# Attention and expert routing in one kernel: where the one-hot operands lie, when the last pair is routed, and how far the list products stand apart

## The chip, the cores and the metric

The kernel runs on one core of a Trainium2 chip. The metric is device time in microseconds (us) of one execution; the span in the profile runs from the first to the last instruction of that execution. The engines are named as in the profile: PE (TensorE), DVE (VectorE), ACT (ScalarE), POOL (GpSimd) and SP (SyncE, which here only issues transfers).

## The reference

Attention over 8 batches, 8 heads, 576 tokens and head size 64: heads 0 to 3 with a local window of 32, heads 4 to 7 with a stride of 32. Its 4608 token rows of 512 go through a mixture of 8 experts, of which each token takes one, and are scaled by its gate.

```python
mask_local = (rel >= 0) & (rel < stride)
mask_strided = (rel >= 0) & (pos[None, :] % stride == pos[:, None] % stride)
...
attn_out = np.matmul(attn, v)                       # softmax under the mask of the head
x = attn_out.transpose(0, 2, 1, 3).reshape(B * S, H * D)
logits = x @ w_gate + modality_bias[modality_id]
e_idx = np.argmax(logits, axis=1)
gate_w = probs[np.arange(N), e_idx]                 # probs: softmax of logits
for e in range(E):
    mask = e_idx == e
    h = np.maximum(x[mask] @ w1[e], 0.0)            # 512 -> 1024
    out[mask] = gate_w[mask, None] * (h @ w2[e])    # 1024 -> 512
```

## The kernel before

**Attention.** The batches are worked on in four pairs (1152 tokens each), each in eight units, local and strided heads in turn. The loop over n emits, for unit n, the scores, for n - 2 the transposes, for n - 3 the products with the values. A local unit writes its heads as columns of the pair's token rows `xt` (128 partitions x 9 x 528 floats, two buffers); a strided unit writes transposed rows `xc2`, `xc3` (two buffers each). `xc0` and `xc1` have one buffer each.

**Routing of a pair** (`after`, `finish_pair`, `route`). When a pair's last unit is done, its local columns are transposed into `xc0`, `xc1` (tiles `xl`, PE and ACT), the gate products run (`lg`), the strided rows are transposed back into `xt` (`xs`), the logits are turned (`lt`), and a chain of small DVE instructions finds expert, gate and rank of each token. Three transfers by SP write the rows with their token number and gate from `xt` to `xd` in memory (L543); the products `rk` give each token a block (`key`) and a place in it (`low`).

**Tables** (`slots`). The expert work is done in slots of 256 tokens of one expert. Phase 0 (2 slots) is built from the first two pairs, phase 1 (4 slots) from three, phase 2 (the other 12 of the 18 fixed slots, a half slot and slots run on demand) from all. For each pair q a `pick` makes one-hot operands: for each of nine token columns a 128 x 128 comparison of `low` with 0..127 (`place`, L702), and the hits of `key` on the slots' keys (`hit`, `tile_no`, L696 and L698, scaled by ACT in L700). Nine products (L718, tile `lists`) then give the token numbers of each slot; `lf` and `li` turn them into whole numbers. In phase 0 the operands lie in tiles of a pool that the expert stage uses later; in phases 1 and 2 in the tags `xc0` to `xc3`.

**Expert slots** (`ffn`). Each slot k has eight steps f of 12 + 6 products. ACT and DVE split the weights `raw` into `wh` and `wl`; the products `o` lag two steps. Before slot k + 1, its rows are gathered by POOL (`gather`, tile `fx`), copied by DVE at f = 1 (`rows`, L837), transposed by transfers on SP (`cols`, L840), copied again at f = 5 (`xs`, L849) and split into `xh`, `xl`. `rows` and `xs` are pinned to program order; so are a few other instructions.

**Order.** Routing and tables are generators in a list `extra`. `pop(k)` advances them by k steps, the oldest first; at `yield LATER` it goes on with the next generator, or ends if there is none. It is called with 5 in each attention step n and with 2 in each step f of a slot but f = 1 and f = 5. In the attention stage PE runs in the order of the program; all else is ordered by a planner, which lets an instruction run as soon as its own model of the times has it ready, the earlier in the program first. A tile with fewer buffers than uses waits until the earlier use is over. Each engine then works through its order without overtaking.

Of the kernel before, what the change touches and what calls it, by code (L numbers as in the profile page):

```python
# [11 lines left out]
F32 = mybir.dt.float32  # L12
F32R = mybir.dt.float32r
BF16 = mybir.dt.bfloat16
# [6 lines left out]
P = 128  # L21
B, H, S, D = 8, 8, 576, 64
STRIDE = 32
NBP = 4
T2 = 2 * S
# [4 lines left out]
SLOT = 256  # L30
# [4 lines left out]
ROW = DM + 16  # L35
WARM = 13
SETUP = 6
POPS, POPF = 5, 2
LT, PK, PL = 7, 2, 2
PT = (9, 9, 5)  # L40
LATER = 1
LAG = 2
SEND, SPLIT = 1, 5
# [131 lines left out]
def attention_moe(ctx: ExitStack, tc: tile.TileContext, a, out):  # L175
# [7 lines left out]
    def pa(name):  # L183
        return ps.tile([P, 512], F32, tag="a", name=name)
# [67 lines left out]
    ap = ap_cm.__enter__()  # L252
    pre_cm = tc.tile_pool(name="pre", bufs=2)
    pre = pre_cm.__enter__()
# [307 lines left out]
    def smalls(shape, dt, name):  # L562
        return cp.tile(shape, dt, name=name)
# [31 lines left out]
    def slots(ph):  # L595
# [4 lines left out]
        bp, n = PHASES[ph]  # L600
        last = ph == len(PHASES) - 1
        tiles = 9 * (bp + 1)
        nk = 2 * n + last
        ct = pa(f"ct{ph}")[:, 0:E]
        nc.tensor.matmul(ct, cb[:, M_ONE:M_ONE + P], cnt[:, bp + 1, :], start=True, stop=True)
        sh = [P, n, E]
# [11 lines left out]
        for sft in (1, 2, 4):  # L618
            t = smalls([P, E], F32, f"inc{ph}{sft}")
# [49 lines left out]
        if not last:  # L669

            t = smalls([P, E], F32, f"tk{ph}")
# [5 lines left out]
            for j in range(2):  # L677
                weights(wi, 0, j, True)

        picks = {}  # L680

        def pick(q, t0, tn):
            if t0 == 0:
                if ph == 0:
                    both = pre.tile([P, 4 * SLOT], F32R, tag=("xh", "xl")[q], name=f"pk{ph}{q}")
                else:
                    c = q if last else q % 2
                    both = ap.tile([P, T2], F32, tag=f"xc{c}", bufs=1 if c < 2 else 2, name=f"pk{ph}{q}")
                both = both.bitcast(BF16)
                picks[q] = (both[:, 0:9 * P].rearrange("p (t c) -> p t c", t=9),  # L690
                            both[:, 9 * P:9 * P + 18 * nk].rearrange("p (t v k) -> p t v k", t=9, v=2))
            place, eq = picks[q]
            ts = slice(9 * q + t0, 9 * q + t0 + tn)
            sh = [P, tn, nk]
            hit, tile_no = eq[:, t0:t0 + tn, 0, :], eq[:, t0:t0 + tn, 1, :]
            nc.vector.tensor_tensor(  # L696
                hit, key[:, ts].unsqueeze(2).to_broadcast(sh), ks.unsqueeze(1).to_broadcast(sh), ALU.is_equal)
            nc.vector.tensor_tensor(  # L698
                tile_no, hit, cf[:, C_V + ts.start:C_V + ts.stop].unsqueeze(2).to_broadcast(sh), ALU.mult)
            nc.scalar.activation(hit, hit, AF.Copy, scale=cf[:, C_P:C_P + 1])  # L700
            for i in range(t0, t0 + tn):
                nc.vector.tensor_scalar(  # L702
                    place[:, i, :], cb[:, M_IO:M_IO + P], low[:, 9 * q + i:9 * q + i + 1], None, ALU.is_equal)

        for _ in range(PK):
            yield LATER
        lists = pa(f"lists{ph}")[:, 0:2 * nk]
        steps = [(q, t0) for q in range(bp + 1) for t0 in range(0, 9, PT[ph])]
        done = 0
        for i in range(len(steps) + PL):  # L710
            if i < len(steps):
                q, t0 = steps[i]
                pick(q, t0, min(PT[ph], 9 - t0))
            yield LATER
            while done <= bp and i + 1 >= PL + sum(q <= done for q, _ in steps) - 1:
                place, eq = picks[done]
                for t in range(9):
                    nc.tensor.matmul(  # L718
                        lists, place[:, t, :], eq[:, t, :, :].rearrange("p v k -> p (v k)"),
                        start=(done == 0 and t == 0), stop=(done == bp and t == 8))  # L720
                done += 1
        lf = smalls([P, nk], F32, f"lf{ph}")
        nc.vector.tensor_scalar(lf[:], lists[:, nk:2 * nk], float(NT), None, ALU.add)
        li = smalls([P, nk], I32, f"li{ph}")
# [187 lines left out]
    for bp in range(NBP):  # L912
        xt = ap.tile([P, 9, ROW], F32, tag="xt", bufs=2, name=f"xt{bp}")
# [6 lines left out]
    tables = {}  # L920

    def after(bp, xt, xcs):
        while bp == NBP - 1 and 1 not in tables:
            yield LATER
        yield from finish_pair(bp, xt, xcs)
        yield
        for ph, (last_bp, _) in enumerate(PHASES):
            if bp == last_bp:
                tables[ph] = yield from slots(ph)
                if ph == 0:  # L930
                    gather(0)
                    yield LATER
                    gather(1)
# [14 lines left out]
    for ph, (bp, n) in enumerate(PHASES):  # L948
        last = ph == len(PHASES) - 1
# [59 lines left out]
    for k, (n, *_) in enumerate(plan):  # L1009
        def between(f):  # L1010
            if f not in (SEND, SPLIT):
                pop(POPF)
            if k + 1 < len(plan):
                if f == SEND:
                    sent[k + 1] = send_tokens(fp, plan[k + 1][0], gathered[k + 1])
                if f == SPLIT:
                    turned[k + 1] = split_tokens(fp, plan[k + 1][0], *sent[k + 1])
            elif f == 3:
                turn(k + 1)
            if f == 4:  # L1020
                gather(k + 2)

        ffn(fp, n, *turned[k], between, partial(load, k + 1))
# [4 lines left out]
    li, _, inc, wall = tables[len(PHASES) - 1]  # L1028
# [38 lines left out]
```

## Time and profile before

| | |
|---|---|
| time, median of 3 runs | 637.94 us (634.6 to 639.87) |
| the profiled execution | 637.19 us, of which span 635.4 us |
| instructions | 15373 |
| PE busy | 592.8 us, 93% |
| DVE busy | 453.0 us, 71% |
| ACT busy | 386.3 us, 61% |
| POOL busy | 191.7 us, 30% |
| mean granted clock of PE | 0.959 |
| moved by DMA | 102.55 MB |

A row of a time line gives start, length, engine, line, operation, output <- inputs, count, and in brackets the idle time before it with what ended it. A row of the waits gives total, number and longest. A row of stretches gives the stretch, its length, the busy time (and count) of PE, PEld, DVE, ACT and POOL, the clock granted to PE (1.00 is full), the share of the DMA engines that was busy, and GB/s. PE's products overlap, so their single lengths add up to more than the time that they take. The attention stage ends at about 171 us; then come 18 slots and the half slot.

### The profile page before, as it was taken

How to read it: one execution, taken by the hardware profiler on the slowest of the kernel's cores; microseconds unless marked ns; L12 is line 12 of the kernel's file. 1: busy time of each engine (PE TensorE's matmuls, PEld its weight loads, DVE VectorE, ACT ScalarE, POOL GpSimd, SP SyncE). 2: the span in 40 equal slices, each digit the busy share in tenths (PEclk: the TensorE clock that was granted, in tenths of full speed). 3: DMA queues.
4: the chain of work that ended last, by engine and by line, in shares of the span. 5: the costliest groups of instructions: out<-in, count | busy, mean ns of one | idle time of the engine just before them, and what ended most of it. 6: DMA issues, size and time to landing. Idle time of an engine off the chain costs nothing.

```text
span 635.4 us, 15373 instructions
## 1 busy us (share of the span) xinstructions
PE 592.8 (93%) x6057; PEld 516.9 (81%) x6057; DVE 453.0 (71%) x1185; ACT 386.3 (61%) x785; POOL 191.7 (30%) x169
## 2 busy tenths in 40 slices
PE   7989989879779978698999999999999999999995
PEld 4778868667668867597998999989999899998985
DVE  7765957847966659956868768777776876877642
ACT  5668677656736645545666666666666666666642
POOL 1010000012034404532553454354244245323311
PEclk9889979959969999889999999999999999999998
DMA  8986996996814487085585485243044148413531
GB/s 310 303 258 197 300 273 209 324 306 178 306 35 136 113 188 246 10 202 143 122 191 185 101 212 186 50 101 76 26 102 101 10 101 242 164 35 67 173 126 53
DMA packets 68079, 102.55 MB, mean 161 GB/s; under 512 B 46431, under 2 KB 47711, under 8 KB 64416
## 3 DMA queue, kind: packets, MB, share of 16 engines
q1 hardware_dynamic: 50848, 52.21, 31.8%
q0 software_dynamic: 16864, 48.83, 24.7%
q8 instruction: 49, 0.80, 0.5%
q10 hardware_dynamic: 288, 0.46, 0.3%
q14 instruction: 30, 0.25, 0.1%
HBM read 123.71 MB, written 19.43 MB: 225 GB/s over the span
## 4 chain that ended last, share of the span: by engine, by line
PE 75%; DVE 10%; DMA 6%; issue 4%; ACT 3%; SPq 0%; POOL 0%; POOLq 0%; DVEq 0%; ACTq 0%
PE h L867 29%; PE o L881 27%; DMA cols<-rows 5%; PE s L307 3%; PE o L339 3%; DVE wl L903 3%; PE ss L394 2%; PE xl L205 2%; PE ot L439 1%; PE t L205 1%; PE lg L485 1%; PE ts L205 1%; DMA qks<-in_qks 1%; PE s L303 1%; PE xs L205 1%
## 5 line engine op out<-in xcount | busy, mean ns | idle before, releaser
L903 DVE TENSOR_TENSOR wl<-raw,wh 128x512 fp32r<-128x512 f32 x288 | 186.9, 687 | 80.5 <-ACT wh L902 80.4
L902 ACT CAST wh<-raw 128x512 fp32r<-128x512 f32 x288 | 163.9, 619 | 94.2 <-PE o L881 94.2
L867 PE MATMUL h<-xh,wh 128*128 128x256 f32 x576 | 166.0, 288 | 5.2 <-ACT xh L854 4.0
L750 POOL DMA_INDIRECT raw<-in_w,wi x72 | 95.0, 1320 | 242.6 <-DVE wl L903 175.4
L867 PE MATMUL h<-xh,wl 128*128 128x256 f32 x576 | 165.2, 287 | 0.6 <-DVE wl L903 0.6
L867 PE MATMUL h<-xl,wh 128*128 128x256 f32 x576 | 164.5, 286 | 0.7 <-DVE xl L855 0.7
L867 PEld LDWEIGHTS h<-xh,wh 128*128 128x128 f32 x576 | 110.6, 192 | 12.6 <-ACT xh L854 4.9
L867 PEld LDWEIGHTS h<-xl,wh 128*128 128x128 f32 x576 | 111.0, 193 | 7.4 <-DVE xl L855 1.2
L881 PE MATMUL o<-wh,hh 128*128 128x512 f32 x288 | 115.6, 401 | 0.4 <-ACT hh L870 0.4
L881 PE MATMUL o<-wl,hh 128*128 128x512 f32 x288 | 113.8, 395 | 0.0
L881 PE MATMUL o<-wh,hl 128*128 128x512 f32 x288 | 113.6, 396 | 0.0
L867 PEld LDWEIGHTS h<-xh,wl 128*128 128x128 f32 x576 | 110.6, 192 | 1.4 <-DVE wl L903 0.8
L870 ACT ACTIVATE hh<-h 128x256 fp32r<-128x256 f32 x144 | 55.3, 384 | 51.2 <-PE h L867 51.2
L872 DVE SCALAR_TENSOR_TENSOR hl<-h,hh 128x256 fp32r<-128x256 f32 x144 | 60.5, 420 | 14.4 <-ACT hh L870 14.4
L881 PEld LDWEIGHTS o<-wh,hl 128*128 128x128 f32 x288 | 54.4, 189 | 12.4
L881 PEld LDWEIGHTS o<-wh,hh 128*128 128x128 f32 x288 | 54.5, 189 | 8.4 <-ACT hh L870 0.6
L881 PEld LDWEIGHTS o<-wl,hh 128*128 128x128 f32 x288 | 54.5, 189 | 5.9
L889 POOL DMA_INDIRECT out<-y,le x36 | 42.8, 1188 | 32.3 <-ACT y L888 25.9
L734 POOL DMA_INDIRECT fx<-xd,li x36 | 41.3, 1148 | 25.3 <-DVE li L725 13.5
L849 DVE COPY xs<-cols 128x1024 uint16<-128x1024 uint16 x34 | 24.4, 769 | 17.5 <-DMA cols<-rows 17.5
L307 PE MATMUL s<-qk,qd 128*64 128x64 f32 x576 | 25.7, 236 | 3.8 <-issue 3.1
L854 ACT CAST xh<-xs 128x512 fp32r<-128x512 f32 x34 | 19.3, 616 | 16.2 <-DVE xs L849 16.2
(182 smaller groups left out, 732.3 us busy)
## 6 DMA issues: line engine op xcount, KB each, us to landing
xd<-xt SPq DMA_DIRECT2D x12, 792.0 KB
qk<-in_qkl SPq DMA_DIRECT2D x16, 592.0 KB
qks<-in_qks SPq DMA_DIRECT2D x16, 576.0 KB
vv<-in_vl SPq DMA_DIRECT2D x16, 520.0 KB
vs<-in_vs SPq DMA_DIRECT2D x16, 288.0 KB
raw<-in_w,wi POOLq DMA_INDIRECT x72, 3.3
vv<-in_vl SPq DMA_DIRECT2D x16, 65.0 KB
fx<-xd,li POOLq DMA_INDIRECT x36, 5.3
```

Source lines behind the costliest of these rows:

```text
L205: nc.tensor.transpose(dst, src, ident)
L307: nc.tensor.matmul(s[64 * jj:64 * jj + 64, g, :], qd[:, i, :, :].rearrange("p b q -> p (b q)"), qk[:, 18 + i:20 + i, :].rearrange("p b q - ...
L734: nc.gpsimd.indirect_dma_start(xt[:, h, :], None, xd[0:xrows, :], IOA(ap=li[:, 2 * s + h:2 * s + h + 1], axis=0))
L750: ins = nc.gpsimd.indirect_dma_start(raws[j].rearrange("p f c -> p (f c)"), None, a["w"], IOA(ap=wi[:, s, j:j + 1], axis=0), bounds_check= ...
L849: pin(nc.vector.tensor_copy(dst, cols[:, :, w].rearrange("p h c q -> p c h q")))
L867: nc.tensor.matmul(hp, w[:, a1], x[:, c, :], start=(k == 0), stop=(k == 11))
L870: nc.scalar.activation(hh[:], hp, AF.Relu)
L872: nc.vector.scalar_tensor_tensor(hl[:], hp, 0.0, hh.bitcast(F32), ALU.max, ALU.subtract)
L881: nc.tensor.matmul(os[h], hx[:, m], w[:, 512:1024], start=(f == 0 and i == 0), stop=(f == 7 and i == 2))
L889: outs.add(nc.gpsimd.indirect_dma_start(out, IOA(ap=le[:, h, 0:1], axis=0), y[:], None, bounds_check=NT - 1, oob_is_err=False))
L902: nc.scalar.copy(wh[:, c], raw[:, c])
L903: nc.vector.tensor_tensor(wl[:, c], raw[:, c], wh[:, c].bitcast(F32), ALU.subtract)
```

## The change

- The operands of `pick` in phases 1 and 2 go into a tile of the tag `xt`, one for the phase, with a stretch of 2304 half-words for each pair; the tags `xc` are not used for them any more.
- `pick` always takes a whole pair (before, phase 2 took five and four columns).
- The last pair's routing no longer waits until table 1 is built.
- `PK`, the rounds of `LATER` between the chain that makes the keys and the first pick, is 2, 2, 7 (was 2); `PL`, the rounds between a pick and its products, is 3, 3, 4 (was 2), and each round of the loop ends with `LATER`.
- The gather for slot 2 is emitted in slot 0 at f = 6 (was f = 4).

Places in the program that follow from these yields:

| step | before | after |
|---|---|---|
| phase 0: products of pairs 0, 1; table | units 26, 27; 28 | units 27, 28; 29 |
| gathers for slots 0, 1 | units 28, 29 | units 29, 30 |
| phase 1: picks of pairs 0, 1, 2 | units 33, 34, slot 0 f0 | the same |
| phase 1: products of pairs 0, 1, 2; table | slot 0 f0, f2, f3; f4 | slot 0 f2, f3, f4; f6 |
| last pair: transposes `xl` | slot 0 f6 to slot 1 f0 | unit 34 to slot 0 f3 |
| last pair: gate products | slot 1 f0 | slot 0 f3 |
| last pair: transposes `xs` | slot 1 f2 to f4 | slot 0 f4 to slot 1 f0 |
| last pair: `lt`, chain, first write to `xd` | slot 1 f6 | slot 1 f2 |
| last pair: other two writes | slot 1 f7, slot 2 f0 | slot 1 f3, f4 |
| last pair: `rk`; keys of phase 2 | slot 2 f0 | slot 1 f4 |
| phase 2: picks | slot 2 f3 to slot 3 f4, eight | slot 2 f6, f7, slot 3 f0, f2 |
| phase 2: products of pairs 0 to 3 | slot 2 f7, slot 3 f2, f4, f7 | slot 3 f3, f4, f6, f7 |
| phase 2: table | slot 4 f0 | slot 4 f0 |

```diff
-LT, PK, PL = 7, 2, 2
-PT = (9, 9, 5)
+LT, PK, PL = 7, (2, 2, 7), (3, 3, 4)
...
-                if ph == 0:
-                    both = pre.tile([P, 4 * SLOT], F32R, tag=("xh", "xl")[q], name=f"pk{ph}{q}")
-                else:
-                    c = q if last else q % 2
-                    both = ap.tile([P, T2], F32, tag=f"xc{c}", bufs=1 if c < 2 else 2, name=f"pk{ph}{q}")
...
+        if ph == 0:
+            room = [pre.tile([P, 4 * SLOT], F32R, tag=t, name=f"pk{t}").bitcast(BF16) for t in ("xh", "xl")]
+        else:
+            big = ap.tile([P, 9 * ROW], F32, tag="xt", bufs=2, name=f"pk{ph}").bitcast(BF16)
+            room = [big[:, 2304 * q:2304 * q + 2304] for q in range(bp + 1)]
...
-        for _ in range(PK):
+        for _ in range(PK[ph]):
             yield LATER
         lists = pa(f"lists{ph}")[:, 0:2 * nk]
-        steps = [(q, t0) for q in range(bp + 1) for t0 in range(0, 9, PT[ph])]
-        done = 0
-        for i in range(len(steps) + PL):
-            if i < len(steps):
-                q, t0 = steps[i]
-                pick(q, t0, min(PT[ph], 9 - t0))
-            yield LATER
-            while done <= bp and i + 1 >= PL + sum(q <= done for q, _ in steps) - 1:
-                place, eq = picks[done]
+        for i in range(bp + 1 + PL[ph]):
+            if i <= bp:
+                pick(i)
+            if i >= PL[ph]:
+                q = i - PL[ph]
+                place, eq = parts(q)
                 for t in range(9):
                     nc.tensor.matmul(
                         lists, place[:, t, :], eq[:, t, :, :].rearrange("p v k -> p (v k)"),
-                        start=(done == 0 and t == 0), stop=(done == bp and t == 8))
-                done += 1
+                        start=(q == 0 and t == 0), stop=(q == bp and t == 8))
+            yield LATER
...
     def after(bp, xt, xcs):
-        while bp == NBP - 1 and 1 not in tables:
-            yield LATER
         yield from finish_pair(bp, xt, xcs)
...
-            if f == 4:
+            if f == (4 if k else 6):
                 gather(k + 2)
```

More of the change, by code (lines that the diff above doesn't have):

```diff
@@ L678, in slots, with parts, pick @@
                 weights(wi, 0, j, True)
-        picks = {}
-        def pick(q, t0, tn):
-            if t0 == 0:
-                if ph == 0:
-                    both = pre.tile([P, 4 * SLOT], F32R, tag=("xh", "xl")[q], name=f"pk{ph}{q}")
-                else:
-                    c = q if last else q % 2
-                    both = ap.tile([P, T2], F32, tag=f"xc{c}", bufs=1 if c < 2 else 2, name=f"pk{ph}{q}")
[L689 to L695, printed above, removed]
+        if ph == 0:
[3 more added lines that the diff above has]
+            room = [big[:, 2304 * q:2304 * q + 2304] for q in range(bp + 1)]
+        def parts(q):
+            return (room[q][:, 0:9 * P].rearrange("p (t c) -> p t c", t=9),
+                    room[q][:, 9 * P:9 * P + 18 * nk].rearrange("p (t v k) -> p t v k", t=9, v=2))
+        def pick(q):
+            place, eq = parts(q)
+            ts = slice(9 * q, 9 * q + 9)
+            sh = [P, 9, nk]
+            hit, tile_no = eq[:, :, 0, :], eq[:, :, 1, :]
             nc.vector.tensor_tensor(
@@ L700, in pick @@
             nc.scalar.activation(hit, hit, AF.Copy, scale=cf[:, C_P:C_P + 1])
-            for i in range(t0, t0 + tn):
+            for i in range(9):
                 nc.vector.tensor_scalar(
                     place[:, i, :], cb[:, M_IO:M_IO + P], low[:, 9 * q + i:9 * q + i + 1], None, ALU.is_equal)
-        for _ in range(PK):
+        for _ in range(PK[ph]):
             yield LATER
         lists = pa(f"lists{ph}")[:, 0:2 * nk]
-        steps = [(q, t0) for q in range(bp + 1) for t0 in range(0, 9, PT[ph])]
-        done = 0
-        for i in range(len(steps) + PL):
-            if i < len(steps):
-                q, t0 = steps[i]
-                pick(q, t0, min(PT[ph], 9 - t0))
-            yield LATER
-            while done <= bp and i + 1 >= PL + sum(q <= done for q, _ in steps) - 1:
-                place, eq = picks[done]
+        for i in range(bp + 1 + PL[ph]):
[3 more added lines that the diff above has]
+                q = i - PL[ph]
+                place, eq = parts(q)
                 for t in range(9):
```

## The prediction

> **What bounds the kernel now.** I read the page first: its engine shares, the granted clock by slices, the chain.
>
> ```profile
> PE 592.8 (93%) x6057; PEld 516.9 (81%) x6057; DVE 453.0 (71%) x1185; ACT 386.3 (61%) x785; POOL 191.7 (30%) x169
> PEclk9889979959969999889999999999999999999998
> PE 75%; DVE 10%; DMA 6%; issue 4%; ACT 3%; SPq 0%; POOL 0%; POOLq 0%; DVEq 0%; ACTq 0%
> ```
>
> PE sets the end, but a quarter of the chain is not PE, and the clock row dips in slices 8 and 11 (127 to 143 us and 175 to 191 us). So the second view was the waits of PE, and the third the time line of PE, for where each of them stands.
>
> ```profile
> PE lists L718 <- ACT pk L700: 13.2, 3, 6.0
> ...
> 128.49 0.34 PE L307 MATMUL s<-qk,qd 128*64 128x64 f32 x5 [2.82 <-issue]
> 133.78 0.38 PE L718 MATMUL lists<-pk 128*128 128x8 bf16 x9 [2.52 <-ACT pk L700]
> 179.77 0.39 PE L718 MATMUL lists<-pk 128*128 128x16 bf16 x9 [4.68 <-ACT pk L700]
> 233.96 0.38 PE L867 MATMUL h<-xh,wh 128*128 128x256 f32 x1 [2.82 <-ACT xh L854]
> 234.76 0.50 PE L881 MATMUL o<-wh,hh 128*128 128x512 f32 x1 [0.42 <-ACT hh L870]
> 241.93 0.19 PE L548 MATMUL rk<-cum,cb_sb 128*128 128x72 bf16 x1 [1.16 <-DVE cum L532]
> 242.68 0.17 PE L605 MATMUL ct<-cnt,cb_sb 128*128 128x8 bf16 x1 [0.55 <-DVE cnt L533]
> 270.13 0.48 PE L718 MATMUL lists<-pk 128*128 128x78 bf16 x5 [5.99 <-ACT pk L700]
> 294.40 0.38 PE L867 MATMUL h<-xh,wh 128*128 128x256 f32 x1 [1.19 <-ACT xh L854]
> 295.52 0.39 PE L867 MATMUL h<-xl,wh 128*128 128x256 f32 x1 [0.74 <-DVE xl L855]
> ```
>
> Almost all that PE loses lies between 124 and 296 us, in places that the tables and the last pair's routing make: a list product once in each phase (2.52, 4.68, 5.99 us), the tokens of slot 2 (2.82, with 0.42, 1.16 and 0.55 behind it) and of slot 4 (1.19 and 0.74). The fourth view, stretches with their clock, shows what each wait costs beyond itself.
>
> ```profile
> 45.00:58.00 13.00, 13.00 (x267) 10.64 (x264) 9.16 (x30) 10.36 (x23) 0.00 (x0) 1.00 0.77 228
> 124.00:147.00 23.00, 17.66 (x273) 14.22 (x275) 12.98 (x62) 11.88 (x27) 5.16 (x6) 0.70 0.98 299
> 130.00:144.00 14.00, 11.47 (x171) 9.87 (x171) 5.58 (x19) 7.83 (x19) 0.85 (x1) 0.52 0.96 318
> 162.00:172.00 10.00, 7.40 (x148) 5.91 (x146) 10.00 (x60) 6.84 (x15) 1.00 (x1) 1.00 0.94 331
> 172.00:181.00 9.00, 3.48 (x25) 3.13 (x26) 8.81 (x34) 5.70 (x13) 4.88 (x2) 0.63 0.29 107
> 181.00:185.00 4.00, 4.00 (x23) 3.96 (x23) 2.74 (x11) 0.74 (x2) 0.00 (x0) 0.56 0.02 0
> 236.00:240.00 4.00, 4.00 (x16) 3.51 (x16) 3.93 (x11) 2.20 (x7) 1.07 (x1) 0.61 0.08 27
> 172.00:295.00 123.00, 105.12 (x710) 92.81 (x710) 85.63 (x261) 64.51 (x136) 45.54 (x30) 0.92 0.55 144
> 270.00:274.00 4.00, 3.87 (x25) 3.82 (x25) 1.54 (x7) 2.77 (x9) 3.39 (x3) 0.59 0.23 51
> 380.00:426.00 46.00, 46.00 (x293) 41.56 (x293) 34.54 (x64) 28.41 (x56) 20.21 (x17) 1.00 0.44 125
> ```
>
> The columns are PE, PEld, DVE, ACT and POOL busy with their counts, the clock, the DMA share and GB/s. Behind each wait PE works at about half clock: (1 - 0.56) x 4 = 1.8, (1 - 0.61) x 4 = 1.6, (1 - 0.59) x 4 = 1.6 us lost. From 296 us on nothing is lost (46.00 of 46.00 busy); there the chain in order of time shows the length of a slot, 22.68 us, or 2.83 for each of its eight steps f:
>
> ```profile
> 366.48 1.44 PE h L867 x12
> ...
> 389.16 1.44 PE h L867 x12
> ```
>
> So the change can only act before 296 us.
>
> **The change part by part, against the profiled execution (637.19 us, span 635.4; the median 637.94 is 0.8 above).**
>
> *1. Table 0's lists go from unit 26 to 27.* The 2.52 us wait at 133.78 goes: its one-hot rows are then a whole unit old. Around it, 124 to 147 us does with 273 matmuls what pair 0's same step did in 13 us with 267, 10 us more; 2.82 of them are the issue stall and stay. Bounds: nothing (DMA is 98% busy there, so loads may take the wait's place) and 10.0 - 2.8 = 7.2. I take -3.0, near the wait's own row, with little for the clock. The Trainium skill ("TensorE: Matmul & The Clock Gate", Part 4) holds that transposes do not count as activity for the gate. By it the 18 transposes that follow in units 26 and 27 would leave the clock low and only the 2.5 would be gained, 0.5 us less in the sum; the 45 to 58 us row, with the same transposes at clock 1.00, speaks against it, and no run here separates the two. The table, and with it the gathers of slots 0 and 1, comes one unit later, before unit 33 needs them: nothing.
>
> *2. Table 1's lists go from slot 0, f = 0, 2, 3 to f = 2, 3, 4.* They stood at 179.77 because the rows were picked late:
>
> ```profile
> 146.12 3.02 DVE L702 TENSOR_SCALAR pk<-cb_sb,low 128x128 bf16<-128x128 bf16 x18 [1.13 <-PE lg L490]
> 176.68 0.37 DVE L696 TENSOR_TENSOR pk<-key,ks 128x72 bf16<-128x72 f32 x2
> 162.47 2.80 SPq L543 DMA_DIRECT2D xd<-xt  x3
> 67.54 2.51 SPq L543 DMA_DIRECT2D xd<-xt  x3
> 79.09 0.20 POOL L538 MEMSET xt<- 128x126 f32 x1 [45.11 <-DMA xd<-xt]
> ```
>
> Gone are the wait of 4.68 and the clock behind it, 1.8: -6.5. What is queued behind the comparisons on DVE is `wl`, and PE waits for that. But the 18 place comparisons that DVE now does at 146 (3.02 us) lie in pair 2's `xt` after the change, and that is free only when its rows have reached `xd`. Pair 0's buffer was free 11.5 us after the first of three writes (67.54 to 79.09); pair 2's, issued at 162.47, then by about 174 (estimate). So 3.0 us of DVE move into a stretch in which it is 10.00 of 10.00 and 8.81 of 9.00 busy, and slot 0's `wl` stands behind them: +3.0. I take -3.5; bounds -6.5 (other gaps take them) and +5.2 (DVE, in order, stands idle for the buffer from the end of the issue, 165.3, to 174: 8.7 + 3.0 - 6.5).
>
> *3. The last pair is routed from unit 34 on, not from slot 0, f = 6.* PE's work is the same; its first nine transposes fall where PE waits for slot 0's weights anyway, and the other transposes and the gate products move from slot 1 into slot 0. ACT's twelve copies move too; ACT is 64.51 of 123 us busy there. What ends is the tail of slot 1:
>
> ```profile
> 208.75 1.07 DVE L702 TENSOR_SCALAR pk<-cb_sb,low 128x128 bf16<-128x128 bf16 x6 [3.67 <-PE lg L490]
> 213.23 1.29 DVE L837 COPY rows<-fx 128x1024 uint16<-128x1024 uint16 x2
> 231.90 1.35 DVE L849 COPY xs<-cols 128x1024 uint16<-128x1024 uint16 x2 [7.22 <-DMA cols<-rows]
> 190.39 0.96 POOL L734 DMA_INDIRECT fx<-xd,li  x1 [0.30 <-issue]
> ...
> DMA to landing us min/median/max: 3.3/3.6/4.6
> ```
>
> DVE stood 3.67 us for the gate products, since table 2's one-hots were to go into `xc0`; then slot 2's rows went out late, at 213.23, and their transposes landed 18.7 us later, so that the stall of 7.22 held all of DVE, the last pair's chain with it. With the one-hots in `xt` the 3.67 goes, and slot 2's rows go out at least that much sooner against PE. Gather 2 is now issued three steps before they are read, 8.5 us, and landed in 3.3 to 4.6: covered. (Uncovered, it would hold DVE at the rows, and so `wl`.) SP's queue gets the last pair's three writes in slot 1 instead of slot 2, behind the transposes of slot 2; slot 2's weights and these transposes share the DMA engines with them, so I leave 2 us of the wait. Of 2.82 + 0.42 + 1.16 + 0.55 + 1.6 of clock = 6.5, -4.5; bounds 0 and -6.5.
>
> *4. Table 2: its chain starts in slot 1, f = 4 (was slot 2, f = 0), seven rounds lie before the picks (were two), the picks are whole, the products four rounds behind.* Before, everything came at once:
>
> ```profile
> 267.23 2.08 DVE L696 TENSOR_TENSOR pk<-key,ks 128x195 bf16<-128x195 f32 x8
> 269.24 2.08 DVE L698 TENSOR_TENSOR pk<-pk,cf_sb 128x195 bf16<-128x195 bf16 x8
> 269.61 2.77 ACT L700 ACTIVATE pk<-pk,cf_sb 128x195 bf16<-128x195 bf16 x8 [3.37 <-DVE pk L698]
> ```
>
> The first product comes in slot 3, f = 3 instead of slot 2, f = 7, four steps or 11 us later against PE, and the chain four steps earlier: 22 us more between them. 5.99 + 1.6 = 7.6; I take -7.0 (bounds 0, if the planner puts the product ahead again, and -7.6). The table is done in slot 4, f = 0 in both, so the gather for slot 6 is where it was. Eight halves become four wholes: four instructions fewer in each of three lines, 1 us of DVE at most, hidden.
>
> *5. Slot 4's tokens:* the wait of 1.19 + 0.74 follows from slot 3 starting with the 5.99; -1.5 of 1.9.
>
> *6. DVE's load in slots 0 to 3* rises by the comparisons that had been done before 172 us: the 18 of part 2, and nine of table 2 for the third pair, which had a free buffer:
>
> ```profile
> 166.48 1.22 DVE L702 TENSOR_SCALAR pk<-cb_sb,low 128x128 bf16<-128x128 bf16 x7
> ```
>
> At 3.02 / 18 = 0.168 each the nine are +1.5. In sum 85.6 + 4.5 = 90.1 us. It also waits for table 2's buffer: if that is the last pair's `xt`, for its writes; +1.0 (bounds 0 and 7.2, the row at 231.90).
>
> Sum: -3.0 - 3.5 - 4.5 - 7.0 - 1.5 + 1.5 + 1.0 = -17.0, so 637.19 - 17.0 = 620.2 by the profiled execution, 620.9 by the median: **621**. As a check, 172 to 295 us shrinks by 14.0 to 109; DVE would be 90.1 / 109 = 83% busy, against 34.54 / 46 = 75% in the undisturbed slots. That is high, and so I go no lower.
>
> **The rivals.**
>
> *All waits go, the clock with them:* -7.2 - 6.5 - 6.5 - 7.6 - 1.9 + 1.5 = -28, 609. For it: all the waits come from late operands, none from PE. Against: DVE would need 90.1 of 102 us.
>
> *The distance is not what the text says, or DVE fills up:* the planner may move the products or picks regardless of the rounds between them; it did comparisons of table 1 at 146 and of table 2 at 208 us, long before their places. Then the waits in front of lists (parts 2 and 4) stay, or come back as DVE's own. What remains is -3.0 - 4.5 + 1.5 + 1.0 = -5, 632 to 633: no change. For it: DVE at 10.00 of 10.00 just where the new work lands.
>
> *Slower: DVE held by the big buffers.* The place is DVE's queue, strictly in order in this trace (231.90). If the planner expects the writes to `xd` early, the first comparison for table 1 stands at 165.3 and holds pair 3's softmax, the chain and slot 0's `wl` until 174: +8.7 + 3.0; the same in slot 2 for the last pair's writes, +7.2 and two half clocks, 3.2; the waits at the lists stay, being behind DVE, and the slot 2 and slot 4 waits too. Only part 1's -3.0 is gained: +19.1, 656; with the first place's 8.7 alone, 646. It decides from the point where DVE's idle time before these comparisons passes about 17 us, which is all I have summed as gains. For it: DVE stood 3.67 us at exactly these comparisons. Against: writes in pair 2 were issued before unit 33, where the first pick has its place.
>
> **How the numbers follow.** Forecast 0.54 (612 to 630), everything goes 0.13, nothing much 0.22, slower 0.11. Below 608 I leave about 0.07 and above 638 about 0.12, so the range is 608 to 638. The three runs spread from 634.6 to 639.87, so about 1% (631.6 to 644.3) is what can be told. Faster by more: 0.54 + 0.13 and a third of the 0.22 = 0.74; within: the rest of it and a little of the slower case, 0.17; slower: 0.09.
>
> **What would show it.** Part 1: no wait at L718 in unit 26, PE through 124 to 147 us in about 20. Part 2: no `lists` wait near 175, the 27 comparisons of table 1 behind the writes to `xd`, PE's first slots set by `wl`. Part 3: `rows` of slot 2 soon after slot 1 starts, the DVE wait for `cols` well under 7.22. Part 4: the eight instructions of 267 to 272 spread as four each, PE without the 5.99. From slot 5 on the old 22.68 us a slot. It would be wrong if the line "lists <- pk" keeps most of its 13.2 us, if DVE shows idle before L702 for `xd`, or if PE waits for `wl` through slots 0 to 3 as long as it did for the lists.

## The result and the profile after

The changed kernel takes 615.13 us (median of 4 runs, 613.9 to 617.41) where the kernel before took 638.9 in the same group (634.6 to 640.74): a ratio of 0.964, 95% interval 0.958 to 0.970. A second group, on another chip, gave 612.72 against 638.92 and 0.962 (0.955 to 0.969). The forecast was 621, range 608 to 638. The profiled execution took 615.41 us, span 613.5, so the span is 21.9 us shorter than before. Ratios leave disturbed executions out and can therefore differ from the quotient of two medians; the profile of one experiment, table 0 nearer, is of a disturbed execution, and only its wait is read.

The page after, the same three lines as before:

```profile
PE 586.9 (96%) x6057; PEld 512.7 (84%) x6057; DVE 453.1 (74%) x1177; ACT 385.3 (63%) x781; POOL 188.9 (31%) x169
PEclk9979979999869999999999999999999999999998
PE 86%; DVE 4%; issue 4%; DMA 3%; ACT 2%; POOL 0%; POOLq 0%; SPq 0%; DVEq 0%; ACTq 0%
```

PE is now 86% of the chain that ended last, DVE 4% instead of 10, DMA 3 instead of 6. Where operands from DVE and ACT still hold PE in the expert slots, its waits say (total, number, longest); no `lists` and no `xh` is left among them:

```profile
PE h L862 <- DVE wl L898: 3.0, 2, 2.4
...
PE h L862 <- ACT wh L897: 0.5, 1, 0.5
```

The stretches, with the columns as before:

```profile
124.00:147.00 23.00, 19.57 (x405) 15.65 (x405) 15.45 (x67) 16.85 (x37) 3.23 (x4) 1.00 0.97 312
172.00:183.00 11.00, 8.56 (x46) 8.09 (x47) 11.00 (x37) 5.25 (x14) 4.94 (x2) 0.53 0.00 1
183.00:295.00 112.00, 112.00 (x786) 99.81 (x785) 94.31 (x257) 70.13 (x143) 49.27 (x39) 1.00 0.60 169
```

From 183 us on PE is busy for 112.00 of 112.00 us at full clock, with DVE at 94.31 / 112 = 84%. What is left behind the attention stage lies at the start of slot 0: 11 us in which DVE is full and the clock stands at 0.53.

To see which slot gained, I take the time line of ACT: the gated output `y` of a slot is its last step. First the kernel before, then the changed one, each with PE's first product of slot 0 ahead of it:

```profile
172.22 0.38 PE L867 MATMUL h<-xh,wh 128*128 128x256 f32 x1 [1.21 <-ACT wh L902]
211.28 1.38 ACT L888 ACTIVATE y<-o,le 128x512 f32<-128x512 f32 x2 [0.26 <-PE o L881]
240.44 1.26 ACT L888 ACTIVATE y<-o,le 128x512 f32<-128x512 f32 x2
263.95 1.27 ACT L888 ACTIVATE y<-o,le 128x512 f32<-128x512 f32 x2
300.64 1.38 ACT L888 ACTIVATE y<-o,le 128x512 f32<-128x512 f32 x2 [0.26 <-PE o L881]
```

```profile
168.84 0.39 PE L862 MATMUL h<-xh,wh 128*128 128x256 f32 x1
209.16 1.26 ACT L883 ACTIVATE y<-o,le 128x512 f32<-128x512 f32 x2
232.46 1.26 ACT L883 ACTIVATE y<-o,le 128x512 f32<-128x512 f32 x2
254.55 1.26 ACT L883 ACTIVATE y<-o,le 128x512 f32<-128x512 f32 x2
278.54 1.38 ACT L883 ACTIVATE y<-o,le 128x512 f32<-128x512 f32 x2 [0.26 <-PE o L876]
```

The differences of neighbouring rows are the slots' lengths. They do not all hold the same work: from the output of slot 2 to that of slot 3 the kernel before does 120 of the products `h`, the changed kernel 96; in slots 0 to 2 it does 288 against 312. So where these two are compared slot by slot, 24 products, two steps f of 1.44 us or 2.9 us in all, have to be counted in slots 0 to 2 instead of slot 3.

The same rows of every run make the table on which the experiments rest (us; ratio to the kernel before with its interval):

| kernel | first product | slot 0 | slot 1 | slot 2 | slot 3 | ratio |
|---|---|---|---|---|---|---|
| before | 172.22 | 39.06 | 29.16 | 23.51 | 36.69 | 1 |
| changed | 168.84 | 40.32 | 23.30 | 22.09 | 23.99 | 0.964 (0.958 to 0.970) |
| changed, again | 166.38 | 39.61 | 23.31 | 22.08 | 24.00 | 0.962 (0.955 to 0.969) |
| table 0 nearer | not read | | | | | 0.972 (0.966 to 0.978) |
| last pair late | 172.83 | 37.47 | 27.09 | 23.61 | 31.64 | 0.983 (0.978 to 0.987) |
| table 2 nearer, both | 175.97 | 36.69 | 23.31 | 33.80 | 22.67 | 0.986 (0.980 to 0.991) |
| table 2, products nearer | 175.21 | 38.98 | 23.31 | 20.88 | 29.51 | 0.969 (0.963 to 0.975) |
| table 2, picks nearer | 170.13 | 38.99 | 23.30 | 31.25 | 22.67 | 0.978 (0.973 to 0.983) |
| table 2 in the columns | 166.75 | 42.21 | 23.89 | 22.36 | 36.17 | 0.997 (0.993 to 1.002) |
| table 1 elsewhere | 175.07 | 34.36 | 23.19 | 22.09 | 24.90 | 0.971 (0.967 to 0.975) |
| table 1 on GpSimd | 164.29 | 39.35 | 40.02 | 22.78 | 23.39 | 0.994 (0.988 to 0.999) |
| table 1, products nearer | 168.15 | 42.58 | 32.46 | 23.47 | 42.32 | 1.018 (1.011 to 1.024) |
| table 1, picks later | 169.35 | 34.96 | 35.09 | 22.82 | 23.24 | 0.970 (0.963 to 0.976) |
| picks later, products kept | 176.86 | 36.34 | 23.30 | 22.09 | 24.00 | 0.969 (0.964 to 0.974) |

Two columns are blurred. Programs that are alike up to there (both of the changed kernel, three of table 2) start slot 0 anywhere from 166.38 to 175.97 us, and take 36.69 to 40.32 for it. The second has a visible cause. The stretch of 16 us from the first product on, in the changed kernel, in its repetition, and in "table 2 nearer, both", whose program is the same there:

```profile
168.84:184.84 16.00, 12.36 (x69) 11.14 (x70) 14.63 (x54) 8.71 (x20) 5.69 (x2) 0.68 0.16 58
```

```profile
166.38:182.38 16.00, 11.93 (x77) 10.53 (x78) 14.63 (x54) 8.72 (x21) 5.68 (x2) 0.79 0.16 60
```

```profile
175.97:191.97 16.00, 12.68 (x117) 10.25 (x118) 14.96 (x50) 10.17 (x24) 6.43 (x3) 1.00 0.18 49
```

The granted clock (third number from the end) is 0.68, 0.79 and 1.00, by execution. What that costs is less than (1 - clock) x 16 us, since the clock is also low where PE stands and waits. In the kernel before, for instance, PE does nothing in these 2 us, at a clock of 0.50:

```profile
176.00:178.00 2.00, 0.00 (x0) 0.00 (x0) 2.00 (x6) 1.10 (x3) 2.00 (x1) 0.50 0.00 0
```

Only the clock that a busy PE lacks costs time. Added up over stretches of half a microsecond, PE's busy time times (1 - clock) is 4.0, 2.8 and 0 us in the 16 us, about what slot 0 differs by (40.32, 39.61 and 36.69 us). Slots 1 to 3 repeat within 0.02 us in the changed kernel's two profiles. For the repetition I had expected the first product at 169 to 172 us and about 10 us of half clock; it came at 166.38, and the half clock lasted 6.8.

### The profile page after: what moved, and what is told of

Same layout as the page of the kernel before. It is cut to its first block, busy times and chain, and to the rows that moved or that the text cites. A ratio compares the mean times of both kernels' runs of the same rounds, so it can differ in the third digit from the quotient of the medians.

```text
span 613.5 us, 15373 instructions
## 1 busy us (share of the span) xinstructions
PE 586.9 (96%) x6057; PEld 512.7 (84%) x6057; DVE 453.1 (74%) x1177; ACT 385.3 (63%) x781; POOL 188.9 (31%) x169
## 4 chain that ended last, share of the span: by engine, by line
PE 86%; DVE 4%; issue 4%; DMA 3%; ACT 2%; POOL 0%; POOLq 0%; SPq 0%; DVEq 0%; ACTq 0%
PE h L862 34%; PE o L876 33%; PE s L306 3%; PE o L338 3%; PE ss L393 2%; PE ot L438 2%; DMA xd<-xt 2%; PE t L204 1%; PE xs L204 1%; PE xl L204 1%; PE lg L484 1%; PE ts L204 1%; DMA qks<-in_qks 1%; PE s L302 1%; DVE pk L700 1%
## 5 line engine op out<-in xcount | busy, mean ns | idle before, releaser
L745 POOL DMA_INDIRECT raw<-in_w,wi x72 | 91.4, 1269 | 221.4 <-DVE wl L898 168.1
L876 PE MATMUL o<-wh,hl 128*128 128x512 f32 x288 | 111.4, 395 | 0.0
L876 PEld LDWEIGHTS o<-wh,hl 128*128 128x128 f32 x288 | 53.4, 188 | 11.5
L884 POOL DMA_INDIRECT out<-y,le x36 | 45.3, 1259 | 27.1 <-ACT y L883 21.0
L729 POOL DMA_INDIRECT fx<-xd,li x36 | 40.0, 1110 | 30.5 <-DVE li L720 14.9
L306 PEld LDWEIGHTS s<-qk,qd 128*64 128x64 f32 x576 | 21.0, 144 | 11.1 <-issue 5.2
L338 PE MATMUL o<-vv,et 128*64 128x65 f32 x512 | 24.9, 244 | 4.6 <-issue 4.6
```

The costliest lines, as they stand in the source:

```text
L306: nc.tensor.matmul(s[64 * jj:64 * jj + 64, g, :], qd[:, i, :, :].rearrange("p b q -> p (b q)"), qk[:, 18 + i:20 + i, :].rearrange("p b q - ...
L338: nc.tensor.matmul(o[64 * jj:64 * jj + 64, k, :], et[:, k, 2 * jj + bb, :, :].rearrange("p g q -> p (g q)"), vv[:, 4 * k + 2 * jj + bb, :] ...
L729: nc.gpsimd.indirect_dma_start(xt[:, h, :], None, xd[0:xrows, :], IOA(ap=li[:, 2 * s + h:2 * s + h + 1], axis=0))
L745: ins = nc.gpsimd.indirect_dma_start(raws[j].rearrange("p f c -> p (f c)"), None, a["w"], IOA(ap=wi[:, s, j:j + 1], axis=0), bounds_check= ...
L876: nc.tensor.matmul(os[h], hx[:, m], w[:, 512:1024], start=(f == 0 and i == 0), stop=(f == 7 and i == 2))
L884: outs.add(nc.gpsimd.indirect_dma_start(out, IOA(ap=le[:, h, 0:1], axis=0), y[:], None, bounds_check=NT - 1, oob_is_err=False))
```

## The experiments

### Distances: table 0

```diff
-LT, PK, PL = 7, (2, 2, 7), (3, 3, 4)
+LT, PK, PL = 7, (2, 2, 7), (2, 3, 4)
```

> The changed kernel with table 0's list products one unit nearer to the picks again (three rounds to two; everything else as changed). Theory: the distance alone took the 2.52 us wait in front of the first lists product away and with it the low clock behind it, so a wait of 2 to 3 us comes back in front of the first lists product in unit 26, the stretch 124 to 147 us shows a granted clock near 0.7 again, the first product of slot 0 comes 3 to 3.5 us later (168.8 to about 172), and the time is 618 to 619 against 615.1. Rival: that stretch is held by the DMA queues (98 per cent busy), the wait only changes its name: 615 within 1 us, first product of slot 0 still at 169.

Measured: 627.54 us, ratio 0.972 against 0.962 to 0.964. The wait is back, at the place where the kernel before had 2.52 us:

```profile
135.19 0.38 PE L713 MATMUL lists<-pkxh 128*128 128x8 bf16 x9 [3.09 <-ACT pkxh L698]
```

So one unit of distance removes it: the profiles with three rounds, on all chips, have none there. Its worth is not settled: 0.8 to 1.0% by the ratios, 5 to 6 us, with intervals that touch. The ratio stands for 621 us beside the first group (0.972 x 638.9), 2 to 3 us more than was expected.

### The last pair late again

```diff
-LT, PK, PL = 7, (2, 2, 7), (3, 3, 4)
+LT, PK, PL = 7, (2, 2, 2), (3, 3, 4)
 def after(bp, xt, xcs):
+        while bp == NBP - 1 and 1 not in tables:
+            yield LATER
```

> The changed kernel with the last pair held back until table 1 is there, as before the change (columns from slot 0, f = 7), and two rounds before table 2's picks, so that its table is done in slot 3, f = 7; one-hots still in the tokens' buffers. Theory: routing the last pair sooner is what freed the way into slot 2, so waits of 3 to 6 us at the tokens of slot 2 come back, the outputs of slots 1 and 2 come 5 to 7 us later, and the time is 620 to 623. Rival: the one-hots' new buffer alone did it (DVE no longer stands 3.67 us for the gate products of the last pair, so slot 2's rows go out in time either way): slot 2 starts as in the changed kernel and the time is 615 to 617.

Measured: 628.99 us, 0.983. Both were wrong about the place. No wait for the tokens of slot 2 came back; here the one-hots' buffer frees them, as the rival said. But the run with table 2 back in the columns, below, has the old buffer and the early routing, and no such wait either: one of the two is enough. The later gather of slot 2, which both runs keep, was not tested alone. Slots 0 to 2 are 2.5 to 3.2 us longer in all (88.17 against 85.71 and 85.00). A busy PE lacks 5.0 us of clock in its first 16 us, against 4.0 and 2.8, and some ten of the last pair's transposes, 0.13 us each, fall here that the changed kernel does ahead of slot 0. And slot 3 is 7.65 us longer, behind a wait for table 2:

```profile
268.96 0.74 PE L713 MATMUL lists<-pk 128*128 128x78 bf16 x9 [6.70 <-ACT pk L698]
```

Four rounds stand between picks and products here too, but only two ahead of the picks. With the same rounds and the early routing (picks nearer, below) the wait is 6.01, and the intervals of the two ratios meet. So at these distances the early routing buys next to nothing; what it gives, by the places in the program, is room for the seven rounds.

### Distances: table 2, three ways

```diff
-LT, PK, PL = 7, (2, 2, 7), (3, 3, 4)
+LT, PK, PL = 7, (2, 2, 2), (3, 3, 2)     # both nearer
+LT, PK, PL = 7, (2, 2, 7), (3, 3, 2)     # products nearer
+LT, PK, PL = 7, (2, 2, 2), (3, 3, 4)     # picks nearer
```

> The changed kernel with table 2 as near as before (two rounds before the picks, products two rounds behind them, wholes), the last pair still routed early, so table 2's products stand in slot 2, f = 2 to 6. Theory: the distance took the 5.99 us wait and the 1.6 us of clock away, since the four hits, tile numbers and copies take 2.8, 0.96 and 2.8 us each on DVE and ACT: a wait of 3 to 6 us in front of the first lists product with 78 columns comes back, 620 to 623. Rival: the early routing is what did it (the chain starts 4 steps sooner, before the rows and splits of slot 2 crowd DVE): the wait stays below 1 us and the time is 615 to 616.

> The changed kernel with table 2's list products two rounds behind the picks instead of four; seven rounds before the picks stay, so the picks stand where they are and only the products move from slot 3, f = 3 to 7, to f = 0 to 4. Theory (both distances are needed, since hits, tile numbers and copies of four pairs take 8 to 9 us one behind another on DVE and ACT): a wait of 3 to 6 us in front of the first lists product with 78 columns, slot 3 longer by as much, 617 to 621 against 612 to 615 of the changed kernel. Rival (the seven rounds alone did it: DVE does the hits ahead of their place as soon as the chain is done, in slot 2, f = 5): no wait at the lists, the time within 2 us of the changed kernel's.

> The changed kernel with two rounds before table 2's picks instead of seven; the products stay four rounds behind the picks, and so come in slot 2, f = 4 to slot 3, f = 0. Theory (the seven rounds put the chain of some thirty small operations on DVE far enough ahead): without them the chain, the hits and the copies follow one another on a DVE that is 84 per cent busy, and a wait of 3 to 7 us comes back in front of the first lists product with 78 columns: 618 to 624. Rival (four rounds between picks and products are enough once the last pair is routed early): no wait, 612 to 616.

Measured: 630.13, 624.55 and 627.76 us. The first product with 78 columns in each, in this order:

```profile
246.06 0.74 PE L713 MATMUL lists<-pk 128*128 128x78 bf16 x9 [8.83 <-ACT pk L698]
```

```profile
261.21 0.49 PE L713 MATMUL lists<-pk 128*128 128x78 bf16 x9 [2.74 <-ACT pk L698]
```

```profile
249.46 0.74 PE L713 MATMUL lists<-pk 128*128 128x78 bf16 x9 [6.01 <-ACT pk L698]
```

Slots 2 and 3 together take 56.47, 50.39 and 53.92 us against 46.08. So the last pair's early routing alone gives none of part 4: with both distances as before, and whole picks, the wait is larger than before (8.83 against 5.99). The seven rounds ahead of the picks carry more (6.1 us, 56.47 to 50.39) than the four behind them (2.6, 56.47 to 53.92), and only both remove it. The places were right and the totals were not: all three lie above what the theories said (620 to 623, 617 to 621, 618 to 624). In the products nearer run the first product came 6 to 9 us later than in the changed kernel's profiles; its wait, 2.74, is a little under the 3 to 6 of its theory, and slots 2 and 3 are 4.3 us longer.

### The buffer: table 2's one-hots back in the columns

```diff
+            if last:
+                room = [ap.tile([P, T2], F32, tag=f"xc{q}", bufs=1 if q < 2 else 2, name=f"pk{ph}{q}").bitcast(BF16)
+                        for q in range(bp + 1)]
+            else:
...
```

> The changed kernel with table 2's one-hots in the four column buffers xc0 to xc3 as before the change (the last pair still sooner, distances as changed). Theory: the change of buffer is what took the 3.67 us stop of DVE for the gate products away (it stood in the middle of the last pair's columns); here table 2's comparisons wait for the last pair's gate products and transposes, which now stand in slot 0, so DVE stands there 1 to 4 us and slot 0 or 1 is longer by 1 to 3 us: 616 to 619. Rival: once the last pair is routed sooner its columns are read long before the comparisons are due, so the buffer makes no difference: the same as the changed kernel within 1 us, no stop of DVE for the gate products.

Measured: 633.57 us, 0.997: nearly the whole gain gone. The small stop of the theory is there, 1.61 us, but PE loses nothing by it: it is busy without a gap from 182 to 209 us. Slot 0 is 2.6 us longer than in the run beside it for another reason. In this kernel DVE does the hits of table 1 behind several `wl`, at 179.50 (172.06 in the run beside it), and PE waits 5.49 us for them. The large loss was in no forecast either. Rows of DVE, PE, DVE, POOL and DVE:

```profile
188.91 3.02 DVE L704 TENSOR_SCALAR pk<-cb_sb,low 128x128 bf16<-128x128 bf16 x18 [1.61 <-PE lg L489]
```

```profile
180.66 0.39 PE L717 MATMUL lists<-pk 128*128 128x16 bf16 x9 [5.49 <-ACT pk L702]
```

```profile
250.35 1.40 DVE L698 TENSOR_TENSOR pk<-key,ks 128x351 bf16<-128x351 f32 x3
```

```profile
250.38 6.80 POOL L749 DMA_INDIRECT raw<-in_w,wi  x1 [4.73 <-DVE wl L902]
```

```profile
281.80 1.35 DVE L848 COPY xs<-cols 128x1024 uint16<-128x1024 uint16 x2 [14.29 <-DMA cols<-rows]
```

The columns of slot 4 landed 14.29 us too late, and slot 3 became 36.17 us long. Ahead of that, a weight gather took 6.80 us to issue while DVE ran table 2's hits (the median of these gathers is 1.0); the next gathers then stood close around the transposes. That this delayed the transposes is a guess.

### DVE at the start of the expert stage

Part 2 of the prediction said that the comparisons stand in front of `wl`. Three kernels take them away from there.

```diff
+            if last:
...
+            else:
+                room = [pre.tile([P, 4 * SLOT], F32R, tag=t, name=f"pk1{t}").bitcast(BF16) for t in ("xh", "xl")]
+                room.append(ap.tile([P, 9 * ROW], F32, tag="xt", bufs=2, name="pk12").bitcast(BF16))
```

> The changed kernel with the one-hots of table 1 for pairs 0 and 1 in the split-token buffers xh and xl (free since table 0), so that only those of pair 2 wait for a token buffer; table 2's as changed. Theory: in the changed kernel some 20 comparisons that wait for xd stand on DVE in front of slot 0's wl, hold PE for 2.42 + 0.54 + 0.59 us and leave it 10.24 us at half clock; with nine in front of it the waits shrink below 1.5 us in all, and if the half clock goes with them (5.1 us) the time is 608 to 612; if the half clock stays, 612 to 614. Rival: DVE is full there in any case (11.00 of 11.00 us in 172 to 183), other work takes the place of the comparisons and wl is as late: 615 within 1 us, 10.24 us of half clock again.

Measured: 620.72 us, 0.971: no gain. All waits for `wl` are gone, but the copies to `xh`, which share the buffers, slid behind eight weight casts on ACT, and PE stood 5.82 us in front of the first product:

```profile
175.07 0.58 PE L866 MATMUL h<-xh,wh 128*128 128x256 f32 x1 [5.82 <-ACT xh L824]
```

```diff
-                nc.vector.tensor_scalar(
+                (nc.gpsimd if ph == 1 else nc.vector).tensor_scalar(
                     place[:, i, :], ...
```

> The changed kernel with the 27 place comparisons of table 1 on GpSimd instead of VectorE. Theory (DVE sets the start of the FFN, the comparisons hold wl back): with none of them on DVE the waits of 2.42, 0.54 and 0.59 us for wl go, DVE has 4.5 us less to do between 169 and 198 us, and slot 0's output comes 3 us sooner, 8 us if the 10.24 us of half clock go too: 607 to 612. Unknown is what a comparison takes on GpSimd; if over 0.5 us each (27 of them: 13.5 us and more), the gathers of weights and the lists products stand behind them and the time is 617 to 625. Rival (the start is held by the weights' casts on ACT, 4.26 us for eight, not by DVE): wl waits turn into waits for wh, 615 within 1 us.

Measured: 631.29 us, 0.994. Again no wait for `wl`. A comparison takes 0.597 us on GpSimd, against 0.168 on DVE:

```profile
L700 POOL TENSOR_SCALAR pk<-cb_sb,low x27: 591/597/6122, 164.5 to 188.7; 128x128 bf16<-128x128 bf16 x27
```

The products waited for them one by one (5.0 us), and in slot 1 the columns of slot 2 came 10.08 us late.

```diff
-LT, PK, PL = 7, (2, 2, 7), (3, 3, 4)
+LT, PK, PL = 7, (2, 3, 7), (3, 3, 4)
-            if f == (4 if k else 6):
+            if f == (4 if k else 7):
                 gather(k + 2)
```

> The changed kernel with table 1's picks one round later (and the gather of slot 2 at f = 7 instead of 6), so that ten comparisons stand in front of the first wl of slot 0 instead of eighteen and the others come between the wl of f = 0 to 3. Theory (DVE in order, wl behind comparisons, is what the start of slot 0 waits for): the waits of 2.2 to 2.4 and 0.6 to 1.3 us for wl shrink to 1 us or less in all, slot 0's first product to its output takes 2 to 3 us less than the 39.6 to 40.3 of the changed kernel, and the time is 1 to 3 us lower, 5 more if the half clock at the start goes too. Rival: the comparisons that come later hold wl of f = 1 to 3 instead, or the rows and transposes of slots 2 and 4 move against the weight gathers and land later, as in the runs with table 1 nearer and with table 2 in the columns (5 to 21 us): 0 to +20 us.

Measured: 624.28 us, 0.970: not faster than the changed kernel. The theory was right about its place and the rival about the rest. The waits for `wl` fell to 0.78 and 0.20 us, and the clock stayed full:

```profile
169.35:185.35 16.00, 14.35 (x126) 11.54 (x127) 15.28 (x56) 11.46 (x27) 4.15 (x3) 1.00 0.33 71
```

Slot 0 takes 34.96 us, 4.7 to 5.4 less than in the changed kernel, but only 1.7 less than the 36.69 with full clock above: the waits are worth some 2 us, the rest is the clock, which this execution may have had by luck. Slot 1 gives more than that back to the columns of slot 2, 35.09 instead of 23.3:

```profile
229.64 1.35 DVE L844 COPY xs<-cols 128x1024 uint16<-128x1024 uint16 x2 [11.12 <-DMA cols<-rows]
```

Their rows were copied at 204.78, and a weight gather was issued beside them at 206.66; in the changed kernel the rows are copied at 209.63, with gathers at 207.44 and 216.19. The later token gather had pushed the weight gathers back in POOL's order. The last run tests that.

```diff
-LT, PK, PL = 7, (2, 2, 7), (3, 3, 4)
+LT, PK, PL = 7, (2, 3, 7), (3, 2, 4)
```

> Table 1's picks one round later as in the run before with ten comparisons in front of the first wl, but its products two rounds behind the picks, so that products, table and the gather of slot 2 (f = 6) stand where the changed kernel has them and GpSimd issues gathers and weight loads in the changed kernel's order. Theory A (the head of the FFN is what the comparisons cost; the 11.12 us stall of slot 1 came from the later gather, behind which the weight loads moved onto the transposes of slot 2): slot 0 in 35 to 37 us from first product to output, no stall of DVE over 4 us for the columns of slot 2, ratio to the kernel before 0.952 to 0.960, about 5 us under the changed kernel. Theory B (a shorter slot 0 moves the transposes against the weight loads whatever the order of issue): the stall of 8 to 12 us is there again, ratio 0.965 to 0.972. A wait of up to 2.5 us at the first lists product with 16 columns is possible in both, since its copy on ACT ended at 179.4 in the run before and the product would come at about 177.

Measured: 619.0 us against 648.66, 0.969 (0.964 to 0.974). Theory A holds for the columns: slot 1 is 23.30 us again, and DVE's longest wait for columns 2.8. Slot 0, 36.34 us (with 1.77 of wait at the first lists product, as allowed for), lies inside its 35 to 37, but so do the 36.69 that the changed kernel's own instructions take at full clock; fewer comparisons ahead of `wl` gain 0.35 us by this. The total is theory B's: the ratio lies above the changed kernel's two, with intervals that meet. The attention stage, alike in this run and the one before, ended 7.5 us later (176.86 against 169.35), and the runs of the kernel before on this chip spread from 636.57 to 661.2. From the first product to the output of slot 3 it needs 105.73 us, the changed kernel 109.70 and 109.00, with clocks of 1.00 against 0.68 and 0.79, which cost a busy PE 4.0 and 2.8 us. So the clock can make nearly all of that difference, and a kernel that beats the changed one was not found.

### Table 1's products nearer

```diff
-LT, PK, PL = 7, (2, 2, 7), (3, 3, 4)
+LT, PK, PL = 7, (2, 2, 7), (3, 2, 4)
```

> The changed kernel with table 1's list products one round nearer to the picks, which puts them into slot 0, f = 0, 2 and 3 as before the change; its one-hots stay in the token buffer. Theory A (the distance is what removed the 4.68 us wait): PE stands again in front of the first lists product with 16 columns, for 3 to 6 us, since its copies on ACT come behind comparisons that wait for xd; 617 to 622 against 615 to 618 of the changed kernel. Theory B (the 4.68 us had not gone but turned into the waits for wl: DVE is the bound of the start of slot 0, and whatever operand comes last has the wait): the lists wait comes back but the waits for wl shrink by about as much, outputs of slot 0 within 1 us of the changed kernel's, and the time is the same within 0.5 per cent.

Measured: 646.37 us, 1.018, slower than the kernel before; neither theory had that. At the start of slot 0 theory A was right:

```profile
172.85 0.39 PE L862 MATMUL h<-xh,wl 128*128 128x256 f32 x1 [4.20 <-DVE wl L898]
178.93 0.39 PE L713 MATMUL lists<-pk 128*128 128x16 bf16 x9 [3.86 <-ACT pk L698]
```

The lists wait came back on top of the wait for `wl`, and slot 0 is 3.0 us longer than in the run beside it. Slots 1 to 3 are another 29 us longer, behind the transposes of slot 2 (8.59 us of DVE's time) and of slot 4, whose rows were copied at 266.87:

```profile
299.02 1.35 DVE L844 COPY xs<-cols 128x1024 uint16<-128x1024 uint16 x2 [21.01 <-DMA cols<-rows]
```

## Why the prediction came out as it did

The direction, the mechanism and the range were right; 5.9 us of gain were missing in the forecast. By the profiles 3.4 us lie ahead of slot 0, 6.0 in slots 0 to 2 (91.73 to 85.71) and 12.7 in slot 3; 0.2 are lost again behind them. With the 24 products `h` counted where they belong, it is 8.9 in slots 0 to 2 and 9.8 in slot 3. The forecasts for these places were 3.0, 8.0 and 8.5, less 2.5 for DVE's load. The gain of part 2 was put too high by 2 to 3 us and that of part 3 too low by some 3.5, and the cost of part 6 did not come; that parts 2 and 3 together are near their sum is luck.

- **Part 1** (-3.0): the wait went, as forecast, and comes back with the old distance. The first product came 3.4 us sooner, which the spread of the attention stage doesn't let one tell from nothing. Nearer to the change it is plainer. From the strided products with the values (`ot`) to the scores (`s`) behind the gate products, the kernel before takes 17.07 us, the changed one 11.22 in both of its profiles; 0.2 of the difference is one pair's list products, which only moved. These are the rows before, then after:

```profile
129.45 1.80 PE L439 MATMUL ot<-eb,vs 72*64 72x72 f32 x32
...
146.52 0.27 PE L303 MATMUL s<-cb_sb 128*128 128x256 bf16 x1
```

```profile
129.51 1.22 PE L438 MATMUL ot<-eb,vs 72*64 72x72 f32 x32
...
140.73 0.27 PE L302 MATMUL s<-cb_sb 128*128 128x256 bf16 x1
```

  The clock of 124 to 147 us rose from 0.70 to 1.00, with the same eighteen transposes in it; so the rule of the Trainium skill that I had set beside it ("TensorE: Matmul & The Clock Gate", Part 4) did not hold the clock down here. Three of the kernels without the wait have a clock of 0.82 to 0.88 there, so the wait is not all that lowers it.
- **Part 2** (-3.5): the term that was mis-sized is the clock. The comparisons cost what I had put down, 3.0: waits of 2.42 and 0.59 us for `wl`, and 0.54 for `wh`, came in the place of 4.68 and 0.62, so 1.75 us were gained. The 1.8 us of clock, counted as gone, did not go with the wait. PE and DVE, in the changed kernel:

```profile
170.91 0.39 PE L862 MATMUL h<-xh,wh 128*128 128x256 f32 x1 [0.54 <-ACT wh L897]
173.84 0.58 PE L862 MATMUL h<-xh,wl 128*128 128x256 f32 x1 [2.42 <-DVE wl L898]
176.94 0.58 PE L862 MATMUL h<-xh,wl 128*128 128x256 f32 x1 [0.59 <-DVE wl L898]
```

```profile
169.26 1.56 DVE L700 TENSOR_SCALAR pk<-cb_sb,low 128x128 bf16<-128x128 bf16 x9 [1.49 <-DMA xd<-xt]
...
171.80 1.39 DVE L700 TENSOR_SCALAR pk<-cb_sb,low 128x128 bf16<-128x128 bf16 x8
173.10 1.28 DVE L898 TENSOR_TENSOR wl<-raw,wh 128x512 fp32r<-128x512 f32 x2
```

  Eighteen comparisons stand before the first `wl`, the first of them held 1.49 us for the writes to `xd`, as the text said; with ten there, the waits for `wl` are 0.78 and 0.20. Over 16 us from the first product on, the kernel before has the same mean clock as the changed kernel in its profile, 0.68, but PE is busy for less of it, 10.70 us against 12.36:

```profile
172.22:188.22 16.00, 10.70 (x77) 9.98 (x77) 12.52 (x45) 7.75 (x17) 4.88 (x2) 0.68 0.26 78
```

  A busy PE lacks 2.8 us of clock there before and 4.0 in the changed kernel (2.8 in its repetition). So part 2 gained 0.5 us in this profile, 1.75 less 1.2, and 1.3 in the repetition.
- **Part 3** (-4.5): of the 8.9 us in slots 0 to 2, part 2 leaves 8.4. The waits at slot 2 are gone whole (4.95 us, of which the forecast left 2), the clock behind them too (1.7), and nine transposes at 0.13 us now run ahead of slot 0 (1.2), which the text named but did not price; 0.5 has no row. The stall of 7.22 us for `cols` is gone. The text named two causes, the early routing and the buffer; the late last pair still had its tokens in time, and so had the early one with the old buffer, so either is enough.
- **Parts 4 and 5** (-8.5): 9.8. The waits of 5.99 and 1.93 went and the 1.6 of clock with them, 9.5 in all, which is the far end of the two ranges; the 1.0 us that the forecast held back was not needed, and 0.3 has no row. The clock was read rightly from its 4 us: the low clock begins earlier, but there PE stands. It is busy for 3.87 of these 8 us, all of it behind 270.13:

```profile
266.00:274.00 8.00, 3.87 (x25) 3.82 (x25) 5.54 (x20) 3.40 (x10) 7.39 (x3) 0.57 0.11 26
```

  The three kernels on table 2 show that both distances were needed.
- **Part 6** (+2.5): nothing. DVE was 84% busy, forecast 83%, and PE lost not a microsecond behind it from 183 us on: a busy DVE had been priced as if it held PE. The nine comparisons for the last pair found room. Phase 2's tile took the buffer that table 1 had left, not the last pair's: its first 27 comparisons run from 191.9 to 198 us, and the last pair's writes to `xd` are issued only at 216.18.
- **The rivals.** The gain of 21.9 us in span lies between the forecast, 17.0, and "all waits go", 28: behind slot 0's start all waits did go, and the objection, a DVE too full, did not hold. DVE stood 1.49 us for the big buffers, so one of the signs of being wrong did show, but far from the 17 that the slower case needed; the writes, issued at 157.77 instead of 162.47, were through 11.5 us later, as estimated. "The distance is not what the text says" did not come: no wait at the lists is left, and the runs with nearer distances, 0.969 to 1.018, bring it back. A slower kernel did turn up among those, by another mechanism: token transposes that land late.

## What to carry to other kernels

Before adding distance, find which of the two is short: the time from the keys to the operands or from the operands to the product; here each alone left 2.7 to 6.0 us of an 8.8 us wait. Price a wait with the clock behind it, but only over the time in which PE is busy: of a low clock under a PE that waits nothing is lost. Before comparing two stretches between the same marks, count whether the same work lies in them. And when an order of transfers works, as here for the token transposes, any shift upstream is tried with an eye on where they land: four kernels lost 10 to 21 us of DVE's time there, whatever else they gained.

## What was unexpected of the hardware

**The landing of token transposes.** From the end of the copy of `rows` to `xs` they took 11.7 us in slot 3 of the changed kernel:

```profile
256.49 1.30 DVE L832 COPY rows<-fx 128x1024 uint16<-128x1024 uint16 x2
...
269.45 1.39 DVE L844 COPY xs<-cols 128x1024 uint16<-128x1024 uint16 x2 [2.15 <-DMA cols<-rows]
```

The same transposes took 23.5 us with table 2 in the columns and 30.9 with table 1's products nearer, and those of slot 2 23.6 with the picks later. Weight gathers were in flight in each case, in the quick ones too; with POOL's order restored, and the products with it, the last of these went. Which neighbourhood slows them is not settled.

**A gather's issue over DVE's hits.** It took 6.80 us with table 2 in the columns, and this in the kernel before, where it began 5.5 us ahead of the hits:

```profile
261.75 10.43 POOL L750 DMA_INDIRECT raw<-in_w,wi  x1 [5.54 <-DVE wl L903]
```

The median of these gathers is 1.0 us in every profile, but at the start of slot 0, with none of table 2's hits, single ones take 2.4 to 4.6, and with table 2's picks nearer one took 1.06 beside the first hits. Spans on POOL are rough, and this wasn't isolated.

**The clock at the start of slot 0.** The same instructions with nearly the same waits ran at 0.68, 0.79 or 1.00. Over the 16 us, 0.68 and 0.79 mean 10.2 and 6.8 us at half clock. The Trainium skill ("TensorE: Matmul & The Clock Gate", Part 1) describes an activity window of 3413 ns that runs freely and isn't tied to the kernel; by that rule the place of the waits in the window decides, and the traces agree as far as these lengths are three and two times that.
